# Down projections with eleven block products for twelve, in five of twelve feed-forward groups

## The chip, the core and the metric

The kernel runs on one core of a Trainium2 chip. A core has TensorE (PE, matrix products into PSUM), VectorE (DVE), ScalarE (ACT), GpSimd (POOL) and SyncE (SP, which issues most DMAs); each works through its own queue in order. The metric is the time of one execution in microseconds of the device.

## What is computed

One transformer block in float32 over 2048 tokens of width 640: layer norm, attention in a sliding window of 256 keys with 32 heads, a residual, then layer norm and a gated feed-forward part of inner width 1536. The change is in the last line:

```
h  = x + attention(layernorm(x)) @ wo
h2 = h + (gelu(n @ w_gate) * (n @ w_up)) @ w_down      # n = layernorm(h)
```

## The kernel before

**Numbers in two parts.** Each float32 operand `a` of a product is kept as two float16 parts, a high one `ah` and a low one `al` (the remainder); the same for the weights, here `dh` and `dl` of the down projection. A product is then ah·dh + ah·dl + al·dh, three float16 products; the last two are the corrections.

**Groups and quads.** The feed-forward part works in groups (c, fg): a chunk c of 512 tokens (four blocks of 128) by a third fg of the inner width (512 = four tiles ft of 128). `ORDER` lists the twelve groups: (0,0), (1,0), (0,1), (0,2), (1,1), (1,2), and then (2,0) to (3,2). From the fourth group on (`PLAIN = 3`), gate and up projection of one tile run as a `quad`, which already computes seven block products for eight. A quad fills one PSUM bank after another in this order: `tp`, `ra` (the gate sum), `pv`, `rb` (the up sum). There is one bank of `tp` and of `pv`, and two each of `ra`, `rb` and `mm`. `quad_out` empties them: ACT copies `tp` to SBUF (`rr` or `gelt`) and POOL adds its halves; DVE adds `rr` or `gelt` to `pv` (row `rs<-pv`), makes the gate sum from `ra` (`gel<-ra`), adds `rb` (`rs<-rb`) and multiplies gate and up (`gel<-rs,ffk,gel`); ACT applies GELU between these and casts the result to `ah`; DVE takes the remainder `al`.

**Down projection before.** `down(c, fg)` computes, for four token blocks b and two column halves of 320, one PSUM sum each in bank `mm`: twelve matmuls of 128 x 128 by 320 columns (four ft by three products). `down_out` adds each sum, scaled, to the row block `ht` of the result on DVE (row `ht<-mm,ffk,ht`). These sums are the filler of the quads: while the quads of one group run, `fill` issues two of the previous group's sums behind each quad. The last group's down projection stands alone at the end.

**Who decides the order.** A planner inside the kernel (`Clock`, `Engine.cost`, `Lane`) gives each instruction an estimated duration and issues whatever its clocks say is ready. So each engine's order is fixed when the kernel is built, and at run time an engine that meets an instruction whose input is late waits there, with all that is queued behind it. All PE work of this stage comes from one generator, `dense_lane`. Other lanes prepare operands: `weight_sums` and `token_sums` make the quads' sums of weights and tokens on DVE and POOL.

## Time and profile before

| | |
|---|---|
| median of three runs | 1002.3 us (1001.79 to 1007.75) |
| the profiled execution, its own time | 1001.09 us |
| its span, first to last instruction | 999.4 us |
| mean granted clock of TensorE | 0.997 |
| PE busy | 982.2 us (98%), 14781 matmuls |
| DVE busy | 747.9 us (75%) |
| ACT busy | 441.8 us (44%) |
| POOL busy | 313.7 us (31%) |

All instructions carry the line of one helper (L199), so rows are told apart by the names of what is written and read: `ht<-mm,ffk,ht 128x320` is the instruction that writes tile ht from mm, ffk and ht. Two busy times of one engine may overlap, since a matmul's modelled end lies behind the start of the next. A row of the view in order of time has start, duration, engine, operation and names, and in brackets how long the engine was idle before it and on whom it waited. The quads run from about 650 us to 980 us, the last down projection from there to 996 us.

### The profile page before, as it was taken

To read this page: it belongs to the slowest core of one execution; us is meant where nothing else is said; L and a number is where in the kernel's file an instruction comes from. 1 tells how busy PE (TensorE), PEld (TensorE's weight loads), DVE (VectorE), ACT (ScalarE), POOL (GpSimd) and SP (SyncE) were. 2 spreads that over 40 slices of the span, in tenths; PEclk is the share of its full clock that TensorE was granted. 3 is DMA by queue.
4 is the path that set the end of the run, shared out by engine and by line. 5 is a ranking of instruction groups with operands and counts; after the bars stand their busy time and mean duration, and the time that the engine had idled before them with its cause. 6 is when DMAs were issued, how large, how long until landed. Compare 5 with 4: busy or idle time off the path is not lost.

```text
span 999.4 us, 34564 instructions
## 1 busy us (share of the span) xinstructions
PE 982.2 (98%) x14781; PEld 715.2 (72%) x14781; DVE 747.9 (75%) x2212; ACT 441.8 (44%) x711; POOL 313.7 (31%) x504
## 2 busy tenths in 40 slices
PE   8999998999999999999999999999999999999998
PEld 7875786787777777777756754577777777777776
DVE  7878998887877876776698697898888874554553
ACT  5615556755565655555577535232212222221220
POOL 7003335543433433333345302164324200000000
PEclk9999999999999999999999999999999999999999
DMA  8667757642432523222315341324544541232211
GB/s 313 124 125 166 174 148 198 152 119 73 113 91 70 104 84 87 63 82 73 113 57 129 60 158 53 123 90 145 155 149 120 158 146 53 80 106 89 72 53 53
DMA packets 129610, 112.92 MB, mean 113 GB/s; under 512 B 85168, under 2 KB 103344, under 8 KB 129456
## 3 DMA queue, kind: packets, MB, share of 16 engines
q1 hardware_dynamic: 117360, 99.97, 36.5%
q10 hardware_dynamic: 12096, 10.75, 3.5%
q8 instruction: 115, 1.88, 0.8%
q14 instruction: 39, 0.32, 0.1%
HBM read 73.73 MB, written 28.84 MB: 103 GB/s over the span
## 4 chain that ended last, share of the span: by engine, by line
PE 78%; DVE 5%; ACT 2%; DMA 1%; issue 1%; SPq 0%; POOL 0%; ACTq 0%; DVEq 0%; POOLq 0%
PE mm L199 37%; PE pv L199 12%; PE ra L199 12%; PE rb L199 10%; PE tp L199 7%; DVE am L199 1%; DVE ts L199 1%; DMA wst<-in_wu_dram 0%; DVE gel L199 0%; DVE ws L199 0%; ACT pt L199 0%; DVE junk L199 0%; DVE ht L199 0%; DMA xt<-in_x_dram 0%; DVE al L199 0%
## 5 line engine op out<-in xcount | busy, mean ns | idle before, releaser
L199 POOL TENSOR_SCALAR_AFFINE_SELECT pt<-pt 128x512 f32<-128x512 f32 x352 | 174.6, 511 | 271.0 <-ACT pt L199 253.2
L199 DVE CUSTOM_DVE_ANT_0 junk<-ra,band 128x320 bf16<-128x320 f32 x230 | 112.5, 489 | 40.5 <-PE ra L199 35.7
L199 ACT ACTIVATE pt<-rb,esc 128x640 f32<-128x640 f32 (+2 forms) x131 | 99.7, 768 | 92.4 <-PE rb L199 73.9
L199 DVE CUSTOM_DVE_ANT_0 junk<-rb,band 128x320 bf16<-128x320 f32 x218 | 106.7, 489 | 34.1 <-PE rb L199 29.0
L199 ACT ACTIVATE pt<-ra,esc 128x640 f32<-128x640 f32 (+2 forms) x125 | 95.0, 767 | 71.1 <-PE ra L199 60.7
L199 PE MATMUL pv<-pt,v 128*21 128x128 f32 x2880 | 103.1, 276 | 0.8 <-ACT oT L199 0.6
L199 PEld LDWEIGHTS <-ah 128*128 128x128 f16 x768 | 75.1, 98 | 28.4 <-issue 1.2
L199 ACT ACTIVATE gel<-gel,ffk 128x512 f32<-128x512 f32 x36 | 26.0, 722 | 136.8 <-DVE gel L199 136.8
L199 PEld LDWEIGHTS <-ws 128*128 128x128 f16 x720 | 70.4, 98 | 9.2 <-DVE ws L199 1.1
L199 PEld LDWEIGHTS pv<-pt,v 128*21 128x21 f32 x2880 | 69.1, 100 | 10.4 <-issue 1.5
L199 PEld LDWEIGHTS <-qT 60*64 60x64 f16 x1280 | 30.0, 104 | 63.4 <-issue 52.4
L199 PEld LDWEIGHTS <-kT 62*64 62x64 f16 x2880 | 64.6, 107 | 10.0 <-issue 6.4
L199 PEld LDWEIGHTS <-gu 128*128 128x128 f16 (+1 forms) x629 | 44.1, 98 | 33.4
L199 DVE SCALAR_TENSOR_TENSOR ht<-mm,ffk,ht 128x320 f32<-128x320 f32 x96 | 52.1, 545 | 15.4 <-PE mm L199 13.4
L199 ACT CAST ah<-gel 128x512 f16<-128x512 f32 x48 | 29.6, 617 | 72.4 <-DVE gel L199 70.8
L199 PE MATMUL mm<-xh,w1h 128*32 128x256 f16 (+1 forms) x356 | 55.9, 273 | 0.9 <-DVE qks L199 0.9
L199 PE MATMUL mm<-xh,w1l 128*32 128x256 f16 (+1 forms) x362 | 56.0, 273 | 0.0
L199 PE MATMUL mm<-xl,w1h 128*32 128x256 f16 (+1 forms) x368 | 55.9, 273 | 0.0
L199 POOL TENSOR_TENSOR gelt<-gelt 128x256 f32<-128x256 f32 x18 | 15.7, 872 | 111.0 <-ACT gelt L199 110.9
L199 PE MATMUL mm<-xl,w0h 128*32 128x256 f16 (+1 forms) x325 | 49.5, 275 | 0.0
L199 PE MATMUL mm<-xh,w0h 128*32 128x256 f16 (+1 forms) x322 | 49.5, 275 | 0.0
L199 PE MATMUL mm<-w3h,ol 128*32 128x320 f16 (+1 forms) x322 | 49.4, 299 | 0.0
(313 smaller groups left out, 2584.9 us busy)
## 6 DMA issues: line engine op xcount, KB each, us to landing
ws<-wsums SPq DMA_DIRECT2D x24, 640.0 KB
qk<-qks ACTq DMA_DIRECT2D x32, 256.0 KB
wsums<-ws SPq DMA_DIRECT2D x12, 640.0 KB
qT<-qk SPq DMA_DIRECT2D x72, 80.0 KB
kT<-qk SPq DMA_DIRECT2D x72, 80.0 KB
ht<-in_x_dram SPq DMA_DIRECT2D x16, 320.0 KB
h_dram<-ht SPq DMA_DIRECT2D x16, 320.0 KB
ht<-h_dram SPq DMA_DIRECT2D x16, 320.0 KB
```

What stands on the lines that cost most here:

```text
L199: r = real(*args, **kw)
```

## The change

The groups `SEVEN = ORDER[6:-1]`, that is (2,0), (2,1), (2,2), (3,0) and (3,1), use `down7` in place of `down`. It takes two token blocks (1, 2) and both column halves (1, 2) together. Written h, l for the two parts of the tokens and d, e for low and high part of the weights, the corrections h·d + l·e of the four results are eight block products; `down7` makes them from seven, with sums and differences of operands:

- of the weights, once per group: t1 = d2 - d1 (POOL), t2 = e2/1024 - t1 (DVE), t3 = t2 - d1 (POOL), t4 = e1 - 1024 t2 (DVE), each 128 x 1280. Rows name them `ts_16076`; the low weights are `w10l`, `w11l`, `w12l`.
- of the tokens, once per pair of blocks: s1 = 1024 l2 + h2 (DVE), s2 = s1 - h1 (POOL), s3 = h1 - h2 (POOL), s4 = l1 - s2/1024 (DVE), each 128 x 512. Rows name them `w9l`, in whose dead space they lie.

A pair is worked in four visits. Two visits stand in each quad: one in the new place `middle`, between the quad's `ra` and `pv`, and one at its end:

- visit 1: m1 = h1·d1 into a bank of `ra`, called x; and h1·e1 + l1·e1 into `mm`, which DVE adds to block 1's first half
- visit 2: s1·t1 into `mm`, called y; and s2·t2 added on top of x
- visit 3: s4·e2 and h1·e2 on top of y, which DVE adds to block 1's second half; and s3·t3 on top of x, which DVE adds to block 2's first half
- visit 4: l2·t4 and h2·e1 into `mm` for block 2's first half; between them h2·e2 on top of x, which DVE adds to block 2's second half

The partial sums are read between additions: x after visits 1, 2 and 3, y after visit 2. The readings after m1, y and x of visit 2 are ACT's (`to_z`, to a buffer z, rows `w8l`), and POOL then adds z to `ht` (row `ht<-ht,w8l`); the others are DVE's (`to_acc`). A pair has 44 matmuls of 320 columns where it had 48. x keeps one of the two `ra` banks from visit 1 to the end of visit 4, that is over two quads. The last group's sums wait until all earlier additions to a block are issued, and the scale of `W["d", fg]` and `UE` are other powers of two, to make room for the sums in float16.

```diff
-UE = -41
+UE = -43
...
-    PLAIN = 3
+    PLAIN, FIRST7 = 3, 6
...
-    def quad(c, fg, ft, fill):
+    def quad(c, fg, ft, fill, middle):
...
         span(gs[:, CW:], s[:, 3], l2, start=False)
+        yield from middle()
         yield pe(s[:, 2], t[:, 2], slots=["pv"])
...
-        yield on("vector", ps)
+        yield on("vector", ps, when=lambda: (c, fg) != ORDER[-1]
+                 or pos["down", c, b] >= 2 * FG - 2)
...
+    N2 = D // 2
+    SEVEN = ORDER[FIRST7:-1]
+    ST = {}
+
+    def seven_weights():
+
+        yield on("gpsimd", when=lambda: pos["quads"] >= FT and W["u", 1].spent
+                 and W["u", 2].spent)
+        t = nc.tile(ffp, [P, KC, 512], F32, "ts0").rearrange("p c n -> p (c n)").bitcast(F16)
+        n = FT * N2
+        t1, t2, t3, t4 = ST["t"] = [t[:, i * n:(i + 1) * n].rearrange("p (f n) -> p f n", n=N2)
+                                    for i in range(4)]
+        ul = [W["u", g].hl[1].rearrange("p c f -> p (c f)") for g in (1, 2)]
+        ST["s"] = [ul[1][:, i * FT * P:(i + 1) * FT * P].rearrange("p (f n) -> p f n", n=P)
+                   for i in range(4)]
+        ST["z"] = [ul[0].bitcast(F32)[:, i * N2:(i + 1) * N2] for i in range(3)]
+        for g, (c, fg) in enumerate(SEVEN):
+            dh, dl = W["d", fg].hl
+            d1, d2, e1, e2 = dl[:, :, :N2], dl[:, :, N2:], dh[:, :, :N2], dh[:, :, N2:]
+            free = lambda n: lambda: pos["visits"] >= 8 * (g - 1) + n
+            yield on("gpsimd", dl, when=free(6))
+            nc.gpsimd.tensor_tensor(t1, d2, d1, op=ALU.subtract)
+            yield on("vector", t1, dh, when=free(6))
+            nc.vector.scalar_tensor_tensor(t2, e2, _pow2(-TE), t1, op0=ALU.mult, op1=ALU.subtract)
+            pos["t", g] = 2
+            yield on("gpsimd", t2, when=free(7))
+            nc.gpsimd.tensor_tensor(t3, t2, d1, op=ALU.subtract)
+            pos["t", g] = 3
+            yield on("vector", t2, when=free(8))
+            nc.vector.scalar_tensor_tensor(t4, t2, -_pow2(TE), e1, op0=ALU.mult, op1=ALU.add)
+            pos["t", g] = 4
+
+    def seven_tokens():
+        yield on("vector", when=lambda: "s" in ST)
+        s1, s2, s3, s4 = ST["s"]
+        for g, (c, fg) in enumerate(SEVEN):
+            yield on("vector", when=lambda: pos["act", c, fg] == FT)
+            ah, al = ga[c, fg]
+            for p in range(2):
+                h1, h2, l1, l2 = (t[:, :, (2 * p + b) * P:(2 * p + b + 1) * P] for t in (ah, al)
+                                  for b in range(2))
+                n = 8 * g + 4 * p
+                yield on("vector", ah, al, when=lambda: pos["visits"] >= n - 2)
+                nc.vector.scalar_tensor_tensor(s1, l2, _pow2(TE), h2, op0=ALU.mult, op1=ALU.add)
+                yield on("gpsimd", s1, when=lambda: pos["visits"] >= n - 2)
+                nc.gpsimd.tensor_tensor(s2, s1, h1, op=ALU.subtract)
+                pos["toks", g, p] = 2
+                yield on("gpsimd", ah, when=lambda: pos["visits"] >= n - 1)
+                nc.gpsimd.tensor_tensor(s3, h1, h2, op=ALU.subtract)
+                yield on("vector", s2, when=lambda: pos["visits"] >= n - 1)
+                nc.vector.scalar_tensor_tensor(s4, s2, -_pow2(-TE), l1, op0=ALU.mult, op1=ALU.add)
+                pos["toks", g, p] = 4
+
+    def down7(c, fg):
+        g = SEVEN.index((c, fg))
+        w = W["d", fg]
+        yield pe(when=lambda: w.ready and w.down and pos["act", c, fg] == FT and c in hts
+                 and len(hts[c]) == CB)
+        (dh, dl), (ah, al) = w.hl, ga[c, fg]
+        d1, e1, e2 = dl[:, :, :N2], dh[:, :, :N2], dh[:, :, N2:]
+        t1, t2, t3, t4 = ST["t"]
+        s1, s2, s3, s4 = ST["s"]
+        k = ffk[:, fg, 2:3]
+        halves = slice(0, N2), slice(N2, D)
+
+        def add(o, l, r, first=False, last=True, more=False):
+            for ft in range(FT):
+                nc.tensor.matmul(o, l[:, ft], r[:, ft], start=first and ft == 0,
+                                 stop=last and ft == FT - 1, skip_group_check=more)
+                pos["dense"] += N2
+                yield
+
+        def to_acc(ps, b, nh, flag=None, name=None):
+            yield on("vector", ps)
+            o = hts[c][b][:, halves[nh]]
+            nc.vector.scalar_tensor_tensor(o, ps, k, o, op0=ALU.mult, op1=ALU.add)
+            if flag:
+                pos[flag] = 1
+            if name:
+                done(name)
+            came(c, b, 0.5)
+
+        def to_z(ps, i, b, nh, flag):
+            yield on("scalar", ps, when=lambda: pos["z", i] == pos["zdone", i])
+            z = ST["z"][i]
+            nc.scalar.activation(z, ps, AF.Copy, scale=k)
+            pos["z", i] += 1
+            pos[flag] = 1
+            yield on("gpsimd", z)
+            o = hts[c][b][:, halves[nh]]
+            nc.gpsimd.tensor_tensor(o, o, z, op=ALU.add)
+            pos["zdone", i] += 1
+            came(c, b, 0.5)
+
+        def when(*reads, flag=None, into=None, slots=(), cond=None):
+            def f():
+                if (flag and not pos[flag] or cond and not cond()
+                        or any(opened[n] >= banks[n] for n in slots)):
+                    return INF
+                t = [nc.ready(reads, "tensor")]
+                t += [nc.slot(psums[n], n, banks[n]) for n in slots]
+                if into is not None:
+                    t.append(nc.others(into, "tensor"))
+                return max(t)
+            return ("tensor",), f
+
+        def go(steps):
+            for _ in steps:
+                yield pe()
+
+        for p in range(2):
+            b1, b2 = 2 * p, 2 * p + 1
+            h1, h2, l1, l2 = (t[:, :, b * P:(b + 1) * P] for t in (ah, al) for b in (b1, b2))
+            f = lambda n: (n, g, p)
+
+            yield when(slots=["ra"])
+            x = bank("ra")[:, :N2]
+            yield from go(add(x, h1, d1, True))
+            tasks.append(to_z(x, 0, b1, 0, f("m1")))
+            yield when(slots=["mm"])
+            ps = bank("mm")[:, :N2]
+            yield from go(add(ps, h1, e1, True, False))
+            yield from go(add(ps, l1, e1, last=True))
+            tasks.append(to_acc(ps, b1, 0, name="mm"))
+            pos["visits"] += 1
+            yield
+
+            yield when(t1, s1, slots=["mm"],
+                       cond=lambda: pos["t", g] >= 2 and pos["toks", g, p] >= 2)
+            y = bank("mm")[:, :N2]
+            yield from go(add(y, s1, t1, True))
+            tasks.append(to_z(y, 1, b2, 1, f("m5")))
+            yield when(t2, s2, flag=f("m1"), into=x)
+            yield from go(add(x, s2, t2, more=True))
+            tasks.append(to_z(x, 2, b1, 1, f("m6")))
+            pos["visits"] += 1
+            yield
+
+            yield when(s4, flag=f("m5"), into=y, cond=lambda: pos["toks", g, p] >= 4)
+            yield from go(add(y, s4, e2, more=True))
+            yield from go(add(y, h1, e2, more=True))
+            tasks.append(to_acc(y, b1, 1, name="mm"))
+            yield when(s3, t3, flag=f("m6"), into=x, cond=lambda: pos["t", g] >= 3)
+            yield from go(add(x, s3, t3, more=True))
+            tasks.append(to_acc(x, b2, 0, flag=f("m7")))
+            pos["visits"] += 1
+            yield
+
+            yield when(t4, slots=["mm"], cond=lambda: pos["t", g] >= 4)
+            ps = bank("mm")[:, :N2]
+            yield from go(add(ps, l2, t4, True, False))
+            yield when(flag=f("m7"), into=x)
+            yield from go(add(x, h2, e2, more=True))
+            tasks.append(to_acc(x, b2, 1, name="ra"))
+            yield from go(add(ps, h2, e1, last=True))
+            tasks.append(to_acc(ps, b2, 0, name="mm"))
+            pos["visits"] += 1
+            yield
+        ga.pop((c, fg))
 
...
-            groups = down(*prev)
-
-            def fill():
-                for _ in range(2):
+            seven = prev in SEVEN
+            groups = (down7 if seven else down)(*prev)
+
+            def fill(n=1 if seven else 2):
+                for _ in range(n):
                     for y in groups:
                         if y is None:
                             break
                         yield y
 
+            def middle():
+                if seven:
+                    yield from fill()
+
             pool = ffpools[ORDER.index((c, fg)) % 2]
             ga[c, fg] = tuple(nc.tile(pool, [P, FT, CB * P], F16, n) for n in ("ah", "al"))
             for ft in range(FT):
-                yield from quad(c, fg, ft, fill)
+                yield from quad(c, fg, ft, fill, middle)
             pos["gu", c] += 1
             prev = (c, fg)
         yield from down(*prev)
```

Three places show what the change moves.

First, POOL during the quads of (2,2) and of every later group. Before, it had one addition per quad:

```order
L199 TENSOR_TENSOR gelt<-gelt 128x256
L199 TENSOR_TENSOR rr<-rr 128x256
```

Now two quads and the start of the next two read, from the first pair's s2 on (`w9l<-w9l,ah` is s2, `w9l<-ah` is s3, `ht<-ht,w8l` the addition of a buffer z):

```order
L199 TENSOR_TENSOR w9l<-w9l,ah 128x512
L199 TENSOR_TENSOR ht<-ht,w8l 128x320
L199 TENSOR_TENSOR w9l<-ah 128x512
L199 TENSOR_TENSOR ht<-ht,w8l 128x320 x2
L199 TENSOR_TENSOR gelt<-gelt 128x256
L199 TENSOR_TENSOR w9l<-w9l,ah 128x512
L199 TENSOR_TENSOR w9l<-ah 128x512
L199 TENSOR_TENSOR rr<-rr 128x256
L199 TENSOR_TENSOR ht<-ht,w8l 128x320
L199 TENSOR_TENSOR ts_16076<-w12l 128x1280
L199 TENSOR_TENSOR ht<-ht,w8l 128x320 x2
L199 TENSOR_TENSOR gelt<-gelt 128x256
```

The second pair's s2 stands behind two additions to `ht` and `gelt`; t1 of the next group (`ts_16076<-w12l`) stands ahead of the second quad's `gelt`, and t3 follows right behind that `gelt`.

Second, DVE over one quad, `rs<-pv` to the second `ht`. Before:

```order
L199 TENSOR_TENSOR rs<-pv,rr 128x512
L199 TENSOR_TENSOR gel<-ra,rr 128x256
L199 TENSOR_TENSOR gel<-ra,rs 128x256
L199 TENSOR_TENSOR rs<-pv,rs 128x256
L199 TENSOR_TENSOR rs<-rb,rs 128x512
L199 SCALAR_TENSOR_TENSOR gel<-rs,ffk,gel 128x512
L199 SCALAR_TENSOR_TENSOR ht<-mm,ffk,ht 128x320
L199 TENSOR_TENSOR al<-gel,ah 128x512
L199 SCALAR_TENSOR_TENSOR ht<-mm,ffk,ht 128x320
```

Now, at the start of a group, from the previous quad's `al` on (the `ts_16076` is t4; `w9l<-al,ah` is s1, `w9l<-w9l,al` is s4):

```order
L199 TENSOR_TENSOR al<-gel,ah 128x512
L199 SCALAR_TENSOR_TENSOR ts_16076<-ts_16076,w12h 128x1280
L199 SCALAR_TENSOR_TENSOR w9l<-al,ah 128x512
L199 SCALAR_TENSOR_TENSOR ht<-mm,ffk,ht 128x320
L199 SCALAR_TENSOR_TENSOR w9l<-w9l,al 128x512
L199 TENSOR_TENSOR rs<-pv,rr 128x512
```

and, from there to the next quad's `rs<-pv`, behind the same `gel`, `rs` and `al` rows:

```order
L199 SCALAR_TENSOR_TENSOR ht<-mm,ffk,ht 128x320
L199 SCALAR_TENSOR_TENSOR w9l<-w9l,al 128x512
L199 SCALAR_TENSOR_TENSOR ht<-ra,ffk,ht 128x320
L199 TENSOR_TENSOR rs<-pv,gelt 128x512
```

The quad's own chain now begins behind t4, s1, a sum of `ht` and s4, and in the second quad behind s4 of the second pair, which reads s2.

Third, PE in visit 4, where the order is printed with its waits:

```order
L199 MATMUL mm<-ts_16076,al 128x320
L199 LDWEIGHTS ah
L199 MATMUL ra<-w11h,ah 128x320 [waits DVE_49]
```

The addition to x (`ra`) waits for DVE's reading of x after visit 3, which is the row `ht<-ra,ffk,ht` above. Before, no matmul of a down projection waited for a reading of its own bank within a sum.

## The prediction

> **What bounds the kernel now.** I read the page first, then the stages in which the change lies, then the chain that ended last.

> ```profile
> span 999.4 us, 34564 instructions
> PE 982.2 (98%) x14781; PEld 715.2 (72%) x14781; DVE 747.9 (75%) x2212; ACT 441.8 (44%) x711; POOL 313.7 (31%) x504
> ```

> PE is busy for 98%, but that is a mean over stages. The stretches of the table below are the quads of one group each (from 836.2 and from 947.1), and ahead of them three early stretches of 20 us:

> ```profile
> 640.00:660.00 20.00, 17.54 (x129) 12.28 (x127) 19.71 (x34) 4.55 (x8) 9.99 (x9) 1.00 0.36 132
> 700.00:720.00 20.00, 20.00 (x151) 14.56 (x149) 16.79 (x37) 4.91 (x8) 7.34 (x7) 1.00 0.48 141
> 740.00:760.00 20.00, 20.00 (x152) 14.60 (x150) 18.38 (x37) 5.11 (x8) 6.49 (x5) 1.00 0.13 51
> 836.20:873.20 37.00, 37.00 (x278) 27.01 (x276) 19.33 (x36) 7.70 (x12) 2.89 (x4) 1.00 0.21 72
> 947.10:984.10 37.00, 37.00 (x276) 26.89 (x275) 19.32 (x36) 7.71 (x12) 2.89 (x4) 1.00 0.11 37
> ```

> The columns are PE, weight loads, DVE, ACT, POOL, granted clock. Where the change works PE has no gap, at clock 1.00, with DVE at 52% and POOL at 8%. So PE time taken away shortens the kernel, as long as the other engines keep up. The chain that ended last shows one quad in its parts and the lone last down projection:

> ```profile
> 970.46 3.26 PE mm L199 x24
> 973.72 1.09 PE tp L199 x10
> 974.82 2.17 PE ra L199 x15
> 976.99 1.09 PE pv L199 x10
> 978.08 1.62 PE rb L199 x10
> 979.70 16.31 PE mm L199 x120
> 996.01 0.03 issue
> 996.04 0.55 DVE ht L199
> ```

> A quad takes 3.26 + 1.09 + 2.17 + 1.09 + 1.62 = 9.23 us, a matmul of 320 columns 3.26/24 = 0.136 us.

> **What is saved.** A pair has 44 matmuls for 48; two pairs in five groups make 40 fewer, so 40 x 0.136 = **5.4 us**. That is all the change can win, 0.5%; a measurement of this kernel tells some 1% from no change. The printed order has these 40 fewer, so that it doesn't do what it says is ruled out.

> **What is added, per group.** Six additions of z to `ht`, four token sums (s2, s3) and t1, t3 on POOL; s1 and s4 twice, t2, t4 and two more sums of `ht` on DVE; six readings on ACT. Sizes come from the nearest rows:

> ```profile
> L199 DVE SCALAR_TENSOR_TENSOR ht<-mm,ffk,ht 128x320 f32<-128x320 f32 x30 | 16.4, 547 | 1.6
> L199 DVE SCALAR_TENSOR_TENSOR gel<-rs,ffk,gel 128x512 f32<-128x512 f32 x15 | 11.3, 751 | 1.6
> L199 DVE TENSOR_TENSOR al<-gel,ah 128x512 f16<-128x512 f32 x15 | 10.4, 692 | 3.3 <-ACT ah L199 3.3
> L199 POOL TENSOR_TENSOR gelt<-gelt 128x256 f32<-128x256 f32 x8 | 5.8, 722 | 68.1 <-ACT gelt L199 68.1
> L199 ACT COPY rr<-tp 128x512 f32<-128x512 f32 x7 | 4.1, 585 | 13.8 <-PE tp L199 13.8
> L199 DVE SCALAR_TENSOR_TENSOR ws<-ws,gu 128x640 f16<-128x640 f16 x4 | 3.2, 812 | 0.0
> L199 DVE SCALAR_TENSOR_TENSOR wst<-wst,h0l x5: 415/425/832, 729.3 to 746.6; 128x256 f16<-128x256 f16 x5
> L199 POOL TENSOR_TENSOR ws<-w5l,w8l x4: 1395/1396/1399, 674.9 to 702.4; 128x640 f16<-128x640 f16 x4
> ```

> DVE's float16 rows give 812 ns at 640 columns and 425 at 256, so about 1 ns a column: 0.67 us for s1 and s4, 1.5 us for t2 and t4. POOL's 1396 ns at 640 gives 1.1 us for s2 and s3 (512) and 2.8 us for t1 and t3 (1280); its 722 ns at 256 gives 0.9 us for an addition to `ht` (320). ACT's reading of 320 columns lies between 585 x 320/512 = 0.37 and 0.585 us; I take 0.42. DVE so gets 4 x 0.67 + 2 x 1.5 + 2 x 0.55 = 6.8 us to its 19.3, POOL 6 x 0.9 + 4 x 1.1 + 2 x 2.8 = 15.4 to its 2.9, in a group of some 36 us. By sums alone all fits. It doesn't by order.

> **Blocking between POOL and DVE.** These rows stand side by side in time:

> ```profile
> 702.36 1.40 POOL L199 TENSOR_TENSOR ws<-w5l,w8l 128x640 f16<-128x640 f16 x1
> 702.42 0.41 DVE L199 TENSOR_TENSOR gel<-ra,rs 128x256 f32<-128x256 f32 x1
> 706.97 1.40 POOL L199 TENSOR_TENSOR ws<-w5h,ws 128x640 f16<-128x640 f16 x1 [3.21 <-DVE ws L199]
> 707.28 1.63 DVE L199 TENSOR_TENSOR al<-gel,ah 128x512 f16<-128x512 f32 x1
> 708.33 1.17 POOL L199 TENSOR_TENSOR rr<-rr 128x256 f32<-128x256 f32 x1
> ```

> `gel<-ra`, with one operand in PSUM, takes its usual 0.41 us beside a running POOL instruction. `al`, with two operands in SBUF, takes 1.63 for 0.69: POOL ends at 708.37, and `al` 0.54 later. POOL's next, `rr`, takes 1.17 for 0.72, so it waited in turn. I read: of two instructions with two SBUF operands each, one per engine, the later waits until the earlier is through. POOL's 2.8 us instructions can then hold DVE for that long, and gel, `al`, s1, s4, t2 and t4 all have two SBUF operands. [...]

> **Where the new waits fall.** Two tight places: the matmuls of visit 4 on x wait for DVE's reading after visit 3; and the next quad's `ra` needs the bank of x, so it waits for DVE's last reading of x. I follow one group from the start of its first quad (0), with PE unhindered and the durations above, and 0.1 to 0.2 us from an end on one engine to a start on another. Visits 1, 3 and 4 have twelve matmuls (1.63 us), visit 2 eight (1.09). Visit 1 begins at 1.09 + 2.17 = 3.3 and its sum is ready at 5.2; `pv` ends at 3.3 + 1.63 + 1.09 = 6.0 and is readable at 6.3; the first quad ends at 6.0 + 1.62 + 1.09 = 8.7.

> First pair, in the printed order of DVE and POOL: `al` of the quad before runs from 1.1 to 1.8 (it began 2.5 us behind its `rb` before, at 982.20 for 979.70; now `rb` lies 1.6 back and one more sum ahead of `al`), t4 until 3.2, POOL's `rr` until 3.9, s1 until 4.6, s2 until 5.8, the addition of m1 until 6.7. DVE's sum of visit 1, ready at 5.2, adds to the same columns and waits for it: until 7.4. s4 waits for s3 (until 7.9), so `rs<-pv` starts at 8.4 for 6.3. GELU follows at 9.9; ACT's two readings of visit 2 stand behind it, until 11.4. POOL does their additions, alternating with gel and `al`, until 13.8, `gelt` until 15.1, and only now the second pair's s2 (16.2) and s3 (17.4). DVE's s4 stands ahead of x after visit 3, waits for both, ends at 18.0, and x is read at 18.5. PE needs it at 8.7 + 3.3 + 1.6 + 1.1 + 1.6 + 0.5 = 16.8: **1.7 us**. The second quad's chain starts at 18.4, x is read for good at 22.0, and `ra` needed it at 20.8: **1.3 us**. A wait of 1.5 us at the start of the group, as the second pair leaves it, moves PE and DVE alike and hardly changes the two: 3.0 together.

> Second pair, from the end of s1·t1 in visit 2 (0): t1 runs until 3.1 and blocks gel, which ends 3.7; addition 4.6, `al` 5.3, addition 6.2, t2 7.6, `gelt` 8.3, `rs<-pv` 8.5 (readable at 6.8). t3 then blocks gel until 11.1, x is read at 12.3, and the next group's `ra` needed it at 10.9: **1.5 us**. The last of the five groups has no t1 to t4 behind it.

> At the end visit 4 covers 1.6 us behind the last `rb` where two sums covered 3.26. DVE's chain of the last quad, from `pv` on:

> ```profile
> 978.18 0.69 DVE L199 TENSOR_TENSOR rs<-pv,gelt 128x512 f32<-128x512 f32 x1 [3.87 <-PE pv L199]
> 979.97 0.69 DVE L199 TENSOR_TENSOR rs<-rb,rs 128x512 f32<-128x512 f32 x1
> 982.20 0.69 DVE L199 TENSOR_TENSOR al<-gel,ah 128x512 f16<-128x512 f32 x1 [0.22 <-ACT ah L199]
> ```

> `al` ends 3.2 us behind `rb` (982.89 - 979.70); with one more sum ahead 3.7. The first sum reads it last at 1.6 + 11 x 0.136 = 3.1, so 0.7 us is lost (0 to 1.3).

> Early, t1 to t4 of the first group fall between 705 and 720, where DVE has 3.2 of 20 us free; plain `down` leaves both `ra` banks to the quads, and PE ran without a gap at 740 with DVE at 92%, so I put nothing (0 to 2). The first group also has the last `token_sums` on DVE; I put no more than a usual group (up to 3).

> **The sum.** -5.4 + 0.7 + 5 x 3.0 + 4 x 1.5 = **+16.3 us**. The profiled execution took 1001.1 us (span 999.4), 1.2 under the median: 1017.4 on its scale, 1018 to 1019 on the median's; I write 1018. Bounds: below, no waits at all, 996.4 and 997.6 on the two scales; above, POOL's instructions each about half a microsecond longer, as `rr` above was, which adds some 6 us over the pairs, and the 5 us of the two unknowns: +27, 1029.

> **Rivals.**
> 1. *The sums come early enough* (not slower). If `rs<-pv` of the first quad starts 1.3 us earlier, GELU is through when visit 2 ends, POOL's two additions run back to back, the second pair's s2 ends before 13 and no wait of the first pair is left; that is the point from which it decides. For it: DVE has 17.7 us free per group in the table, and quads ran without a gap at 740 with DVE fuller than it will be here. Against it: the path t4, s1, s2, addition, sum is serial over two engines, and with one `ra` bank for the gate the slack is some 0.2 us. Waits of 0 to 5: 997 to 1003 on the median's scale.
> 2. *Half the waits*: those behind s4, or those behind t1 and t3, but not both; net -5.4 + 0.7 + 6 to 15: 1003 to 1012.
> [...]

> **Chances.** Forecast (1012 to 1029) 0.56; first rival 0.14; second 0.22; third and worse 0.08. The range 999 to 1029 leaves out some 0.08 below and 0.08 above. Faster by over 1% would need twice the whole saving: 0.01. Within 1%: 0.35. Slower by over 1% (above 1012): 0.64.

> **What would show it.** Right: per-group stretches of 39 to 41 us for 36.95, PE waiting for DVE `ht` at `ra` and in visit 4, gel and `al` rows of over 1 us beside POOL's `ts` rows. Wrong: stretches of 35.9 us with PE at 100%, as in the first rival; POOL's 1280-column rows well under 2.8 us; s4 finding s2 done; or PE waiting for something not named here, such as ACT's readings.

## The result, and the profile after

| | median | runs | span of the profiled execution |
|---|---|---|---|
| before | 1001.43 us (999.98 to 1007.75) | 9 | 999.4 us |
| after | 1009.06 us (1006.98 to 1012.79) | 9 | 1006.8 us |

The ratio is 1.0063, 95% interval 1.0042 to 1.0083: the change makes the kernel 0.6% slower. The medians differ by 7.6 us and the two spans by 7.4, where 16.3 were forecast: the direction was right, the size a good twice too large. 1009 lies in the interval of the second rival, half the waits. The head of the page of the changed kernel, to be held against 999.4 us and 982.2, 747.9 and 313.7 us before:

```profile
span 1006.8 us, 34669 instructions
PE 979.4 (97%) x14741; PEld 710.5 (71%) x14741; DVE 808.8 (80%) x2252; ACT 454.8 (45%) x741; POOL 402.1 (40%) x564
```

PE is busy 2.8 us less and the span is 7.4 us longer, so PE now waits. The stretches of the first four of the five groups, each from the first matmul of its first quad to the next group's (columns: PE, weight loads, DVE, ACT, POOL, granted clock, DMA):

```profile
799.11:839.29 40.18, 37.88 (x271) 26.82 (x269) 36.50 (x65) 10.04 (x19) 20.53 (x16) 0.96 0.33 106
839.29:875.92 36.63, 36.02 (x270) 26.21 (x268) 29.30 (x43) 9.70 (x18) 20.59 (x16) 1.00 0.22 73
875.92:913.88 37.96, 36.20 (x270) 26.13 (x268) 31.11 (x45) 10.22 (x19) 19.90 (x17) 1.00 0.23 81
913.88:951.86 37.98, 36.20 (x270) 26.14 (x268) 31.14 (x45) 10.23 (x19) 19.93 (x17) 1.00 0.27 95
```

Before, each took 36.96. With eight matmuls fewer (8 x 0.136) a group without waits would take 35.87. So the groups lose 4.31, 0.76, 2.09 and 2.11 us; the fifth, by its quads (951.86 to the last quad at 980.60, where the same took 26.63 without waits in an experiment below), 2.11. What PE waits for in that stretch:

```profile
PE ra L199 <- DVE gel L199: 4.9, 4, 2.1
PE ra L199 <- DVE ht L199: 3.4, 5, 0.8
PE mm L199 <- DVE al L199: 0.3, 1, 0.3
```

All of it is DVE, as forecast; but the larger part is a wait of `ra` for `gel`, a gate sum, and not for a reading of x. In the fourth group PE's rows are these:

```profile
924.77 1.25 PE L199 MATMUL ra<-h1h,w5h 128*128 128x512 f16 x5 [0.94 <-DVE gel L199]
...
932.85 0.70 PE L199 MATMUL ra<-w10h,ah 128*128 128x320 f16 x4 [0.84 <-DVE ht L199]
...
935.02 1.24 PE L199 MATMUL ra<-h1h,w5h 128*128 128x512 f16 x5
```

The first is `ra` of the second quad, the second visit 4 on x, the third `ra` of the third quad, which waits for nothing. DVE and POOL at the start of the same group:

```profile
916.91 0.89 POOL L199 TENSOR_TENSOR rr<-rr 128x256 f32<-128x256 f32 x1 [2.63 <-ACT rr L199]
917.13 2.02 DVE L199 SCALAR_TENSOR_TENSOR ts<-ts,w10h 128x1280 f16<-128x1280 f16 x1
919.07 0.68 DVE L199 SCALAR_TENSOR_TENSOR w9l<-al,ah 128x512 f16<-128x512 f16 x1
919.83 1.15 POOL L199 TENSOR_TENSOR w9l<-w9l,ah 128x512 f16<-128x512 f16 x1 [2.03 <-DVE w9l L199]
920.93 0.86 POOL L199 TENSOR_TENSOR ht<-ht,w8l 128x320 f32<-128x320 f32 x1
921.83 0.55 DVE L199 SCALAR_TENSOR_TENSOR ht<-mm,ffk,ht 128x320 f32<-128x320 f32 x1 [2.08 <-POOL ht L199]
922.30 1.16 DVE L199 SCALAR_TENSOR_TENSOR w9l<-w9l,al 128x512 f16<-128x512 f16 x1
923.38 0.68 DVE L199 TENSOR_TENSOR rs<-pv,rr 128x512 f32<-128x512 f32 x1
```

This is the chain that the prediction followed: t4 (2.02 us, held by POOL's `rr`), s1, s2 on POOL, POOL's addition of m1, DVE idle for 2.08 us until that is through, the sum of visit 1, s4 (1.16 us, held by POOL's s3), and `rs<-pv` 9.5 us after the group's start (8.4 forecast).

The first group loses 3.9 of its 4.31 us in its fourth quad, at another place than the rest:

```profile
825.85 2.61 POOL L199 TENSOR_TENSOR ts<-w11l 128x1280 f16<-128x1280 f16 x1 [1.70 <-PE mm L199]
826.47 2.26 DVE L199 SCALAR_TENSOR_TENSOR ts<-h1l,h1h 128x256 f16<-128x256 f16 x1
829.45 1.82 PE L199 MATMUL ra<-h0h,w5h 128*128 128x512 f16 x5 [2.06 <-DVE gel L199]
829.90:833.30 3.40, 3.40 (x15) 2.01 (x14) 2.60 (x3) 2.25 (x5) 2.59 (x3) 0.51 0.00 0
```

POOL's t1 of the next group holds one of DVE's token sums for 2.26 us in place of 0.41, the quad's gate sum comes late, PE waits 2.06 us, and the last row, a stretch of 3.4 us from 829.90, has a granted clock of 0.51: the fifteen `ra` matmuls took 3.75 us for 2.17.

### The profile page after: what moved, and what is told of

Same layout as the page of the kernel before. It is cut to its first block, busy times and chain, and to the rows that moved or that the text cites. A ratio compares the mean times of both kernels' runs of the same rounds, so it can differ in the third digit from the quotient of the medians.

```text
span 1006.8 us, 34669 instructions
## 1 busy us (share of the span) xinstructions
PE 979.4 (97%) x14741; PEld 710.5 (71%) x14741; DVE 808.8 (80%) x2252; ACT 454.8 (45%) x741; POOL 402.1 (40%) x564
## 4 chain that ended last, share of the span: by engine, by line
PE 69%; DVE 10%; POOL 2%; issue 2%; ACT 2%; DMA 2%; ACTq 0%; SPq 0%; DVEq 0%; POOLq 0%
PE mm L199 33%; PE ra L199 12%; PE pv L199 11%; PE rb L199 8%; PE tp L199 6%; DVE ts L199 2%; DVE gel L199 1%; DVE ht L199 1%; DVE w9l L199 1%; DVE rs L199 1%; POOL w9l L199 1%; POOL ht L199 1%; DVE am L199 1%; ACT pt L199 1%; DVE al L199 1%
## 5 line engine op out<-in xcount | busy, mean ns | idle before, releaser
L199 POOL TENSOR_SCALAR_AFFINE_SELECT pt<-pt 128x512 f32<-128x512 f32 x352 | 175.1, 513 | 269.2 <-ACT pt L199 251.6
L199 DVE CUSTOM_DVE_ANT_0 junk<-ra,band 128x320 bf16<-128x320 f32 x230 | 112.5, 489 | 39.7 <-PE ra L199 34.9
L199 ACT ACTIVATE pt<-rb,esc 128x640 f32<-128x640 f32 (+2 forms) x131 | 99.9, 769 | 92.3 <-PE rb L199 75.9
L199 DVE CUSTOM_DVE_ANT_0 junk<-rb,band 128x320 bf16<-128x320 f32 x218 | 106.7, 489 | 34.3 <-PE rb L199 29.3
L199 ACT ACTIVATE pt<-ra,esc 128x640 f32<-128x640 f32 (+2 forms) x125 | 95.1, 768 | 70.2 <-PE ra L199 60.7
L199 PE MATMUL pv<-pt,v 128*21 128x128 f32 x2880 | 103.3, 276 | 0.8 <-ACT oT L199 0.6
L199 ACT ACTIVATE gel<-gel,ffk 128x512 f32<-128x512 f32 x36 | 26.0, 721 | 155.0 <-DVE gel L199 155.0
L199 PEld LDWEIGHTS <-ah 128*128 128x128 f16 x648 | 63.4, 98 | 28.6 <-issue 5.6
L199 PEld LDWEIGHTS <-ws 128*128 128x128 f16 x720 | 70.6, 98 | 10.5 <-DVE ws L199 1.1
L199 PEld LDWEIGHTS pv<-pt,v 128*21 128x21 f32 x2880 | 69.0, 100 | 10.6 <-issue 1.3
L199 PEld LDWEIGHTS <-qT 60*64 60x64 f16 x1280 | 30.0, 104 | 64.3 <-issue 54.2
L199 PEld LDWEIGHTS <-kT 62*64 62x64 f16 x2880 | 64.2, 106 | 10.7 <-issue 7.3
L199 DVE SCALAR_TENSOR_TENSOR ht<-mm,ffk,ht 128x320 f32<-128x320 f32 x86 | 46.4, 543 | 31.2 <-POOL ht L199 18.0
L199 PEld LDWEIGHTS <-gu 128*128 128x128 f16 (+1 forms) x629 | 44.0, 98 | 34.6 <-DVE gel L199 1.2
L199 ACT CAST ah<-gel 128x512 f16<-128x512 f32 x48 | 29.6, 617 | 76.0 <-DVE gel L199 74.4
L199 PE MATMUL mm<-xh,w1h 128*32 128x256 f16 (+1 forms) x356 | 55.9, 273 | 1.3 <-DVE qks L199 1.3
L199 PE MATMUL mm<-xh,w1l 128*32 128x256 f16 (+1 forms) x362 | 56.0, 273 | 0.0
L199 PE MATMUL mm<-xl,w1h 128*32 128x256 f16 (+1 forms) x368 | 55.9, 273 | 0.0
L199 DVE TENSOR_TENSOR al<-gel,ah 128x512 f16<-128x512 f32 x48 | 43.3, 902 | 11.1 <-ACT ah L199 11.1
L199 PE MATMUL mm<-w3h,ol 128*32 128x320 f16 (+1 forms) x322 | 49.4, 299 | 0.0
L199 PE MATMUL mm<-w3h,oh 128*32 128x320 f16 (+1 forms) x310 | 49.4, 299 | 0.0
L199 PE MATMUL mm<-w3l,oh 128*32 128x320 f16 (+1 forms) x319 | 49.3, 299 | 0.0
```

The lines of the kernel that those rows point to most:

```text
L199: r = real(*args, **kw)
```

## The experiments

Theory 1 going in was: DVE's in-order chain is late in the first quads of each group, held up by POOL, and PE pays for this lateness wherever it first needs DVE; the second pair's holds (by t1 and t3) cost PE nothing. Rivals: A, too few banks of `ra`; B, DVE simply has too much work; C, POOL's rate; D, the two engines do not hold one another. In the table the numbering of the groups is the changed kernel's. The plain group ahead of the first takes 36.95 or 36.96 us in every trace but t4_later's (37.58, where the moved t4 makes PE wait already), so tenths of a microsecond can be compared; the ratios are to the kernel before on the same chip, and kernels without one ran once, for their trace.

| kernel | first | second | third | fourth group, us | time, us | ratio (95%) |
|---|---|---|---|---|---|---|
| before | 36.96 | 36.96 | 36.95 | 36.96 | 1001.43 | 1 |
| after | 40.18 | 36.63 | 37.96 | 37.98 | 1009.06 | 1.0063 (1.0042 to 1.0083) |
| ra_three_banks | 38.36 | 38.29 | 37.98 | 37.99 | 1009.89 | 1.0058 (1.0035 to 1.0082) |
| dve_reads_x | 36.77 | 35.87 | 35.91 | 35.91 | 998.55 | 0.9961 (0.9942 to 0.9980) |
| t4_later | 37.74 | 39.19 | 40.55 | 40.55 | 1015.28 | 1.0121 (1.0096 to 1.0147) |
| t1_t3_in_four | 37.41 | 38.14 | 37.35 | 37.34 | 1006.80 | 1.0035 (1.0015 to 1.0055) |
| m1_by_dve | 37.81 | 36.79 | 36.79 | 36.79 | 1002.75 | |
| m56_by_dve | 38.10 | 36.24 | 36.33 | 36.34 | 1000.94 | |
| t4_once | 38.49 | 36.38 | 36.24 | 36.23 | 1001.67 | |
| t1_t3_once | 36.65 | 37.94 | 36.45 | 36.59 | 1002.21 | |
| t4_early | 46.44 | 40.21 | 41.05 | 40.89 | 1022.34 | |
| four_groups | 36.96 | 35.87 | 36.63 | 37.98 | 1000.78 | |
| six_groups_dve | 38.81 | 36.61 | 35.87 | 35.91 | 1009.12 | |
| dve_reads_x_split | 36.78 | 35.87 | 35.87 | 35.87 | 997.90 | 0.9963 (0.9950 to 0.9976) |

**A third bank for `ra`.** 

```
-        banks.update(ra=2, rb=2)
+        banks.update(ra=3, rb=1)
```

> Theory 1 (DVE's in-order chain is late by itself, held up by POOL): a third `ra` bank takes away the 0.93 us that the second quad's `ra` waits in each of the last groups, but DVE reads x after visit 3 no earlier, so the wait in visit 4 grows from 0.9 to about 1.8 us; groups stay at 38.0 us and the time within 1 us of the changed kernel (1008 to 1010). Rival A (too few banks of `ra`): the 0.93 us are gone in three or four groups and visit 4 still waits 0.9: groups of 37.0 us, 1005 to 1006.

The fourth group and PE's waits:

```profile
915.51:953.50 37.99, 36.19 (x270) 26.20 (x268) 31.14 (x45) 10.22 (x19) 19.94 (x17) 1.00 0.28 94
PE ra L199 <- DVE ht L199: 8.1, 6, 1.8
```

The waits for `gel` are gone, the one in visit 4 has grown from 0.84 to 1.8 us, and the group is as long as before to 0.01 us. All of this was expected. So the bank decides where PE waits and not how long; rival A falls. DVE and POOL together took 38.0 us for such a group with two banks and with three.

**DVE reads x itself.**

```
-            tasks.append(to_z(x, 0, b1, 0, f("m1")))
+            tasks.append(to_acc(x, b1, 0, flag=f("m1")))
```

and the same for the readings of y and x behind visit 2.

> The six partial sums read between additions are added to `ht` by DVE straight from PSUM (0.55 us each); ACT's six copies and POOL's six additions a group are gone. Theory 1: POOL is out of the chain between visit 1 and `rs<-pv`, which starts some 1.4 us earlier, and both waits of the steady groups (0.93 and 0.9 us) go or nearly go: groups of 36 to 36.6 us, 1003 to 1006. Rival B (DVE simply has too much work): with 3.3 us more a group, 34.4 of 36, DVE falls further behind and groups grow beyond 38 us, 1010 to 1016.

```profile
911.42:947.33 35.91, 35.91 (x270) 26.15 (x268) 31.68 (x51) 7.31 (x12) 13.69 (x10) 1.00 0.28 94
PE ra L199 <- DVE ht L199: 0.7, 1, 0.7
```

PE is busy for the whole group and both waits are gone, though DVE has more to do (31.68 us in 35.91 for 31.14 in 37.98): rival B falls for these groups. This kernel is 0.4% faster than the one before, and its time lies 4.5 us below the expected range, above all since the first group too lost only 0.90 us for 4.31. The outcome is that of the prediction's first rival, "the sums come early enough", but not by its condition: `rs<-pv` starts at 8.4 us (919.84), just where the forecast had it and not 1.3 us earlier, yet x is read after visit 3 from 15.8 to 16.4 (927.25), and PE takes it up at 16.9 without a wait.

**One half of it at a time.** The first reading of a pair alone on DVE, or the two behind visit 2 alone:

```
m1_by_dve:  to_z(x, 0, b1, 0, ...)  ->  to_acc(x, b1, 0, ...)
m56_by_dve: to_z(y, 1, b2, 1, ...), to_z(x, 2, b1, 1, ...)  ->  to_acc(...)
```

> Of the three partial sums read between additions, the first of a pair (m1, behind visit 1) goes to DVE straight from PSUM; the other two (behind visit 2) stay with ACT and POOL. Theory 1: `rs<-pv` of the first quad starts at 8.2 to 8.6 us after the group's start instead of 9.5, the second quad's `ra` no longer waits; POOL's two additions behind visit 2 still hold s2 and s4, and visit 4 waits 0.3 to 1.4 us: steady groups 36.2 to 37.4 us for 38.0. If visit 2's additions alone matter (rival): 38.0.

> The other half: the two readings behind visit 2 go to DVE, the first of a pair stays with ACT and POOL. Theory 1: `rs<-pv` stays at 9.3 to 9.6 us and the second quad's `ra` still waits 0.8 to 1.0 us; s2, s3 and s4 of the second pair come early and visit 4 no longer waits: steady groups 36.8 to 37.1 us. If the reading behind visit 1 alone matters (rival): 38.0 less nothing at visit 4, 37.8 to 38.2.

```profile
910.42:947.21 36.79, 36.20 (x270) 26.12 (x268) 32.34 (x47) 9.19 (x17) 18.98 (x15) 1.00 0.29 98
909.52:945.86 36.34, 36.12 (x271) 26.13 (x268) 30.77 (x49) 8.34 (x14) 15.12 (x12) 1.00 0.27 94
PE ra L199 <- DVE gel L199: 2.3, 4, 0.6
```

Each wins more than half of the 2.1 us by itself, 1.19 and 1.64. The length of the first is inside its expectation, but its waits stand elsewhere: `rs<-pv` comes at 9.14 us and not by 8.6, the second quad's `ra` still waits 0.58 us (the last row, of m1_by_dve), and visit 4 waits for nothing. The second is better than expected: with POOL's two additions behind visit 2 gone, DVE is less late at the end of the group, and the second quad's wait shrank to 0.2 us too. Parts of one lateness do not add up.

**t4 moved.** Two visits later, behind the first quad's `gel`:

```
-            yield on("vector", t2, when=free(8))
+            yield on("vector", t2, when=free(10))
```

> t4 (2.0 us on DVE at the start of each steady group, ahead of s1) is issued two visits later, behind `gel` of the first quad. Theory 1: s1 and all behind it start 1.5 to 2 us earlier, `rs<-pv` of the first quad at 7.5 to 8 us for 9.5, and the second quad's `ra` no longer waits; the same 1.5 to 2 us now stand ahead of the second pair's s1, so the wait in visit 4 stays at 0.8 to 1.5: groups of 37.0 to 37.6, 1005 to 1008. Rival C (POOL's rate sets it, not DVE's order): groups of 38.0, 1009.

```profile
936.36 0.70 PE L199 MATMUL ra<-w10h,ah 128*128 128x320 f16 x4 [2.66 <-DVE ht L199]
```

Half right. The second quad's `ra` waits 0.2 us, as expected (`rs<-pv` at 8.6 us, less early than hoped), but visit 4 waits 2.66 us and not 0.8 to 1.5. The groups are 2.6 us longer; of these the waits make 1.1, and the rest is a stretch of half clock behind this wait (granted 0.50 from 937.5 to 940.9). t4 now runs beside POOL's two additions behind visit 2, takes 2.15 us, and these take 3.47 us for 2.41 before; s2 and s4 of the second pair stand behind both. The same 1.5 us of work cost more in the new place because of what ran beside it.

t4 a group earlier, into a second buffer, right behind t2:

```
-            yield on("vector", t2, when=free(8))
+            yield on("vector", t2, when=free(7))
+            t4 = ST["t4", g] = t4s[g % 2]
```

> t4 gets a second buffer (alternating by group) and is issued in the group before, right behind t2 in the second pair, ahead of DVE's reading of x after visit 7; otherwise the changed kernel. Theory 1: t4, two SBUF operands, waits until POOL is through t3 (2.6 us) and then takes 1.5; DVE reads x 3 us late, and the second pair's visit 4 waits 2.5 to 3.5 us; in return the first pair starts without t4. Steady groups 38.5 to 39.5 us for 38.0. If instructions of the two engines did not hold one another (rival D), t4 would end 1.5 us behind t2, visit 4 of the second pair would wait about 1.2 us and the first pair's waits would go: 36.8 to 37.3.

The second buffer lies over a part of w8h that the quads still read, so their weights are no longer the reference's, and one `rb` of the first group waits 5.0 us for that writing; the first group's length is not used.

```profile
961.36 0.54 DVE L199 SCALAR_TENSOR_TENSOR ht<-mm,ffk,ht 128x320 f32<-128x320 f32 x1
961.58 2.60 POOL L199 TENSOR_TENSOR ts<-ts,w11l 128x1280 f16<-128x1280 f16 x1 [1.50 <-DVE ts L199]
961.82 3.71 DVE L199 SCALAR_TENSOR_TENSOR ts<-ts,w11h 128x1280 f16<-128x1280 f16 x1
965.45 0.54 DVE L199 SCALAR_TENSOR_TENSOR ht<-ra,ffk,ht 128x320 f32<-128x320 f32 x1
966.04 0.70 PE L199 MATMUL ra<-w10h,ah 128*128 128x320 f16 x4 [3.18 <-DVE ht L199]
```

This is the holding in one view. t3 begins on POOL while `ht<-mm`, with an operand in PSUM, runs unhindered; t4, with two SBUF operands, begins 0.24 us later and takes 3.71 us for 1.48: it ends 1.35 us behind t3. DVE's reading of x is 3 us late and PE waits 3.18 us. Rival D falls. The third and fourth group came out at 41.05 and 40.89 us and not 38.5 to 39.5, since half clock came with two of the three waits (granted 0.50 from 882.1 and from 926.5).

**t4, or t1 and t3, left out** of the later groups:

```
+            if g == 0:
                 nc.vector.scalar_tensor_tensor(t4, t2, ...)        # t4_once
+            if g == 0:
                 nc.gpsimd.tensor_tensor(t1, d2, d1, ...)           # t1_t3_once, and t3 alike
```

> t4 is computed in the first group of seven alone; in the four later ones the instruction is left out, so their fourth visit adds the first group's t4. Theory 1: the 2.0 us of t4 go from the head of DVE's chain, `rs<-pv` starts at 7.5 to 8.1 us, and both waits go or nearly go: steady groups 35.9 to 36.5 us for 38.0. Rival C (POOL's additions set the end, wherever DVE stands): 37.4 to 38.0.

> t1 and t3 (POOL, 1280 columns) are computed in the first group alone and left out in the four later ones, whose t2 and t3 so have stale values. The prediction gave their blocking of DVE's gel 1.5 us of TensorE's time a group: steady groups would be 36.5 us. Theory 1: gel takes 0.75 us for 2.72, and TensorE gains nothing by it, since none of its matmuls waited there: 37.7 to 38.1 us.

```profile
910.48:946.71 36.23, 36.20 (x270) 26.12 (x268) 29.98 (x44) 10.23 (x19) 21.10 (x17) 1.00 0.30 99
910.28:946.87 36.59, 36.03 (x270) 26.22 (x268) 29.37 (x45) 10.33 (x18) 16.93 (x14) 1.00 0.25 82
```

t4_once came as expected in length, with `rs<-pv` at 8.6 us for 7.5 to 8.1, and rival C falls. t1_t3_once did not: theory 1 gave the second pair's holds nothing, the prediction gave them 1.5 us a group, and they are worth 1.4 to 1.5. Where that is paid shows in DVE's first `rs<-pv` ahead of the group's start and in t4 behind it, first in the changed kernel (start 951.86), then without t1 and t3 (start 910.28):

```profile
950.35 0.67 DVE L199 TENSOR_TENSOR rs<-pv,gelt 128x512 f32<-128x512 f32 x1
...
907.30 0.69 DVE L199 TENSOR_TENSOR rs<-pv,gelt 128x512 f32<-128x512 f32 x1 [0.61 <-PE pv L199]
...
912.07 1.48 DVE L199 SCALAR_TENSOR_TENSOR ts<-ts,w10h 128x1280 f16<-128x1280 f16 x1
...
918.38 0.68 DVE L199 TENSOR_TENSOR rs<-pv,rr 128x512 f32<-128x512 f32 x1
```

With t1 and t3, DVE starts that sum 1.51 us ahead of the group's start; without, 2.98 ahead, and it waits for PE there. So the second pair leaves DVE 1.47 us late. No matmul of the second pair or of the next group's first `ra` needs DVE in that time; the lateness is carried into the next group, where t4 starts at 3.25 us (917.13) for 1.79, `rs<-pv` at 9.50 for 8.10, and PE pays in its second quad. Theory 1 was wrong on this point and is mended: the holds of both pairs make one lateness, and PE pays it once a group, at the first places that need DVE.

The second groups bear this out without any further change. They begin with DVE more or less late, by what the first group did to it (changed kernel, start 839.29; then t1_t3_in_four, start 835.78):

```profile
836.30 0.69 DVE L199 TENSOR_TENSOR rs<-pv,gelt 128x512 f32<-128x512 f32 x1
...
834.43 0.67 DVE L199 TENSOR_TENSOR rs<-pv,gelt 128x512 f32<-128x512 f32 x1
```

DVE starts this sum 2.99 us ahead of the group in the first and 1.35 in the second, and the groups lose 0.76 and 2.27 us. The steady groups of the changed kernel (1.52 ahead, 2.1 lost), those of t1_t3_in_four (2.16, 1.48) and the second group of ra_three_banks (1.21, 2.42) fall on the same line: each microsecond that DVE comes later costs PE one.

**t1 and t3 in pieces.**

```
-            nc.gpsimd.tensor_tensor(t1, d2, d1, op=ALU.subtract)
+            for i in range(FT):
+                nc.gpsimd.tensor_tensor(t1[:, i], d2[:, i], d1[:, i], op=ALU.subtract)
```

> t1 and t3 each in four POOL instructions of 320 columns instead of one of 1280 (0.86 us each for 2.61). Theory 1: in the first group of seven, the token sums behind t1 wait at most 0.9 us instead of 1.85, the 2.06 us wait of the fourth quad's `ra` falls to 0.3 to 1.2 and the stretch of half clock behind it (1.6 us lost) does not come: first group 36.8 to 38 us for 40.2, steady groups 38.0 as before, 1005.5 to 1007. Rival B (DVE has too much work there anyway, however long one hold is): first group 39.5 to 40.5 us, 1009.

```profile
798.37:835.78 37.41, 36.20 (x270) 26.14 (x268) 33.99 (x63) 9.87 (x18) 20.22 (x21) 1.00 0.35 115
911.27:948.61 37.34, 36.21 (x271) 26.15 (x268) 29.75 (x45) 10.23 (x18) 21.99 (x23) 1.00 0.27 93
```

The first group is 2.8 us shorter, at clock 1.00, as expected: the wait of the fourth quad's `ra` fell from 2.06 to 0.63 us, so there it was the length of one hold (without t1, in t1_t3_once, that group takes 36.65). The other half of the gain, some 1.7 us, is the half clock that did not come; t4_once, whose first group has the same work, also had none, behind the same wait of 2.06 us, and took 38.49. The later groups gained 0.6 that the expectation had not, since shorter holds leave DVE less late (the point above); the second group lost 1.5, since DVE entered it late, as shown above. With DVE reading x as well:

> DVE reads all partial sums straight from PSUM (as in dve_reads_x), and t1 and t3 come in four POOL instructions of 320 columns each. Theory 1: the steady groups stay at 35.9 us, which is all that 264 matmuls of a group need; the 0.9 us that the first group loses in dve_reads_x stand in the visit on x behind the first group's second quad, in DVE's token sums and not behind t1, so it keeps 36.3 to 36.9 us: within 1 us of dve_reads_x, 997.5 to 999 beside a kernel before of 1001 to 1003. If the long POOL instructions still cost anything, 0.5 to 1 us less.

The steady groups are at 35.87, without a wait, and the first at 36.78: the medians of 997.90 and 998.55 us, each beside its own runs of the kernel before, tell the two apart no further than their ratios, 0.9963 and 0.9961.

**Fewer and more groups.** `FIRST7` = 7 in the changed kernel and 5 in dve_reads_x:

> Four groups of seven products, the first one plain again. Theory 1: the first group's 4.3 us of waits come from the token sums that share DVE with it, so the plain group takes 36.95 us for 40.2 and the later ones stay as they are (36.6 to 38.0): 3 us less from the first group's start to the end than the changed kernel. If the first group of seven pays 4 us wherever it stands (rival): the next group takes 40 us and nothing is won.

```profile
834.93:870.80 35.87, 35.87 (x271) 26.21 (x268) 26.69 (x40) 9.32 (x17) 20.32 (x16) 1.00 0.22 72
870.80:907.43 36.63, 36.22 (x270) 26.05 (x268) 29.67 (x45) 10.34 (x19) 20.57 (x17) 1.00 0.26 85
907.43:945.41 37.98, 36.21 (x271) 26.14 (x269) 31.14 (x45) 10.21 (x19) 19.92 (x17) 1.00 0.27 93
```

The plain group takes 36.96 as expected, but the next, now the first of seven, loses nothing at all: DVE starts its `rs<-pv` 4.61 us ahead of it, and uses this reserve up. The three groups behind it lose 0.76, 2.11 and, up to the last quad (945.41 to 972.80), 0.76 us again. Lateness that grows does not explain this, since DVE enters all three alike, 1.51 or 1.52 us ahead. Their DVE order differs: in the first and the third of them t4 stands ahead of `al`, where POOL's `rr` does not hold it, and `rs<-pv` ahead of s4; in the second it is the changed kernel's. The two rows of t4 (starts 870.80 and 907.43):

```profile
873.44 1.48 DVE L199 SCALAR_TENSOR_TENSOR ts<-ts,w12h 128x1280 f16<-128x1280 f16 x1
...
910.67 2.02 DVE L199 SCALAR_TENSOR_TENSOR ts<-ts,w10h 128x1280 f16<-128x1280 f16 x1
```

`rs<-pv` so starts at 8.54 us and 9.49 us. The 0.76 us of the changed kernel's second group have another cause: its order is the usual one, but PE's half clock in the first group let DVE catch up (in t4_once, with the same wait of 2.06 us at full clock, DVE starts the `rs<-pv` ahead of that group 1.35 us early and not 2.99), and t4 starts 1.78 us behind the group's start (841.07 for 839.29). From the first group to the last quad four_groups is 6.7 us shorter than the changed kernel, twice what was expected.

> As dve_reads_x, with a sixth group by seven products, the one ahead of the five (eight matmuls fewer, 1.1 us). It shares DVE with the token sums of two quads more. Theory 1: DVE has no room there (92% busy at 740 us in the kernel before), so that group loses 1 to 4 us to waits and nothing is won: the stretch of the last six groups 0 to 3 us longer than in dve_reads_x. If the room is enough: 1.1 us shorter.

The sixth group took 44.05 us (763.26 to 807.31) for the 36.96 of a plain one, 8.2 lost for the 1 to 4 expected, and the group behind it 38.81 for 36.77: from its start to the last quad 9.8 us longer than dve_reads_x, three times the upper end of what was expected. DVE is busy for 38.06 of the 38.81 us ahead of 807.31, and two waits of 2.29 and 2.85 us stand there.

```profile
768.50:807.31 38.81, 32.62 (x231) 22.44 (x229) 38.06 (x64) 6.89 (x11) 19.21 (x15) 0.96 0.42 128
```

## Why the prediction was wrong in size

- **The saving** was right: 1.09 us a group, as the groups of 35.87 us show, 5.4 in all.
- **What is added** was right in kind and size: t1 and t3 2.61 us (2.8), s2 and s3 1.15 (1.1), an addition 0.86 (0.9), s1 0.68 (0.67), t2 and t4 1.48 (1.5) where nothing holds them (2.0 in a steady group, where POOL does); ACT's reading 0.51 to 0.53 (0.42).
- **Blocking** was right, and t4_early shows it by itself (t4 3.71 us for 1.48 beside t3). The forecast gel rows of over 1 us beside POOL's `ts` are there (942.77, 2.72 us).
- **The first failing step** is "the next quad's `ra` needs the bank of x, so it waits for DVE's last reading of x". It carried 1.3 us of the first pair and all of the second pair's 1.5, 12.5 of the 21.0 us of waits in the sum. The third quad's `ra` starts at 935.02 while DVE reads x for the last time until 936.49: it took the bank that the second quad's gate sum had left. The quad that shares a bank is the second, with the first quad's gate sum, and it waits 0.94 us there.
- **The second failing step** is that delays were added up which are one and the same. "A wait of 1.5 us at the start of the group, as the second pair leaves it, moves PE and DVE alike and hardly changes the two": PE did not wait there, DVE's 1.47 us stayed with DVE, and made up most of the first pair's lateness. A steady group so loses 2.1 us, with ra_three_banks nearly all of it in visit 4 (1.8), for the forecast 1.7 + 1.3 + 1.5 = 4.5. That t1 and t3 are worth 1.4 to 1.5 us, as forecast, is half luck: DVE's lateness was sized rightly, but where PE pays it was not. The second rival's time came about in the same way: not one kind of hold without the other, but both in one lateness.
- **The first pair's own chain** was too long: without the carried part s4 ends at 17.0 us and x is read by 17.5 (t1_t3_once), where 18.0 and 18.5 were forecast, which leaves 0.6 to 0.7 us lost and not 1.7. `rs<-pv` came 0.3 us earlier than forecast (8.10 for 8.4), POOL's additions behind visit 2 were through at 13.15 us for 13.8, and its `gelt` took 0.72 us for the 1.3 that had been put, all in t1_t3_once.
- **The first group** was put down as a usual one of 4.5 us, and cost 4.31: right by accident. The cause, a token sum held by t1, a wait of 2.06 and half clock, is none of the terms; the half clock, some 1.7 us of it, came here alone and in no steady group (granted 1.00 in their rows), and by the line of the second groups most of that came back there, since DVE caught up meanwhile.
- **The tail**: 0.7 forecast; from the last quad's start to the end it took 26.2 us for 25.84, so 0.36.

The sum with the measured terms, in spans: -5.45 saved, 4.31 + 0.76 + 2.09 + 2.11 + 2.11 = 11.38 lost, 0.36 at the tail, and 1.1 that lie ahead of the first group (799.11 for 798.01): +7.4, which is 1006.8 - 999.4. The 1.1 are no cost of the change: 1.04 of them are there at the start of a quad at 660.47 us (659.43 before), some 50 us ahead of t1, and from there to the first group both kernels take 138.6 us. So nothing was lost early, as the prediction had put it.

What stays open: each kernel was traced in one execution, so how often the half clock of the first group comes in the other runs is not known. The second group depends on it: where it did not come (t1_t3_in_four, t1_t3_once), DVE entered that group 1.4 to 1.6 us later than in the changed kernel, and it was 1.3 to 1.5 us longer.

## What to carry to other kernels

When an in-order engine falls behind in several places of a loop, follow its lateness round the loop as one quantity: it grows, is carried where nobody waits, and is paid once, where the other engine next needs it; adding up each place's wait counts it twice (here 1.47 us, which the second pair left on DVE, inside the 2.1 us that a steady group lost). If DVE and POOL both work from SBUF and hold one another, as t4 and t3 did (3.71 us for 1.48), try having DVE read PSUM directly, even if it is the busier one: here three readings a pair at 0.55 us on DVE beat three copies and three additions on two other engines, and turned +0.6% into -0.4%. A long POOL instruction costs what stands behind it on DVE (here t1, 2.61 us, held a token sum for 2.26 us in place of 0.41, and PE waited 2.06), so ask what that is, and not what DVE's share is.
